# A retention layer and a wave MLP in one kernel: the whole instruction order redone, and q's scaling moved to the copy of x for six more units

## The chip, the cores and the metric

The kernel runs on one core of one Trainium2 chip. The metric is the device time of one execution in microseconds. Three executions of the kernel before gave 170.76, 172.34 and 173.16 us; the median is 172.34.

## The reference

`q`, `k`, `v` have the shape (4 batches, 8 heads, 768 tokens, 64) in float32. The first part is a recurrent retention, the second a mixing layer over its output:

```python
for t in range(S):                       # retention, gamma per head
    state = gamma * state + outer(k[t], v[t])
    y[t] = scale * (q[t] @ state)
x = y, heads side by side                # (4, 768, 512)
theta = x @ w_theta
zr, zi = x * cos(theta), x * sin(theta)
u = x + w_tok_r @ zr + w_tok_i @ zi      # over the 768 tokens of a batch
out = u + maximum(u @ w_ch, 0)
```

## The kernel before, in words

**Retention.** The work is cut into 24 units: unit n is one batch (n // 6), 256 tokens (the pair of 128-token chunks i = n // 2 % 3 of the batch) and four of the eight heads (h = n % 2). `Lk`, `Lq`, `Lv` (L159) load 256 KB each in float32, from SP's queue or ACT's as the last letter says (s or a), into 16 buffers for k and q and 9 for v. The decay is split: v is multiplied by gamma^-position when it is copied to bf16 (`cv`, L310), and the other factor, gamma^position times the scale, goes on q or on x. `ck` and `cq` are plain copies to bf16; `cqs` (L304) is the copy of q that scales it. If q was scaled, the result is copied to `xT` as it is (`XB`, L141 on DVE and L139 on ACT); if not, `XA` (L443, DVE alone) scales it there.

`Tk`, `Tq` (PE transposes, L318) with the copy `E`, or one DMA-transpose `Dk` (L334), give `kqT`. `A` (L348) is k.q within the 256 tokens, `m` (L357) its mask, `Y` (L425) the product with v, `ST` (L375) the unit's k.v sum, `S0` and `S1` (L393, L397) add it to the running state, `SB` copies the state to bf16 (`sbd`), and `I` (L413) applies the state of before to q. Units of one head half and batch depend on each other through the state.

**Mixing.** Two units give the `xT` of two 128-token chunks C = 0 to 23. `Tx` with the copy `Ex`, or a DMA-transpose `Dx` (L464), turns it to `x_sb`; `Hh` (L471) is x @ w_theta, `CN` (L478) its sine and cosine on ACT, `z` (L485) the two products. The six chunks of a batch must be there before `M` is complete: `M.t.s0` (L511) adds chunk s0 to the output tile t, two matmuls of 512 columns each. `u` (L518) adds x, `Tu` with `Eu`, or a DMA-transpose `Du` (L533), turns u, `O` (L538) multiplies by w_ch, `f` (L544) finishes the tile in one of four buffers, and `SO` (L549) stores it. The last tile is split in two halves (`Mh`, `uh`, `Tuh`, `Euh`, `Oh`, `fh`, `SOh`). The two token matrices are loaded by POOL in three groups of row blocks each (`Pw.r.g`, L184: block 0, blocks 1 and 2, blocks 3 to 5), and transposed on PE (`Tw.r.block`, L493) with the copy `Ew`; `Pth` and `Pch` load w_theta and w_ch. `Z` are matmuls on zeros whose result nobody reads; `const1` to `const9` and `constA` make tables, masks and the sine's table load (`const7`).

**What sets the order.** Nothing is scheduled at run time but by data. `ORDER` is a written list of 925 steps; the kernel calls them one after the other, and each engine (PE, DVE, ACT, POOL and SP, which issues transfers) executes its own instructions of them in that order. A step with a last letter p, v, a or s goes to POOL, DVE, ACT or SP's queue. A step waits until what it reads is there and its buffer is free, and all that stands behind it on the same engine waits with it. DMA-transposes are all issued by SP. The transfers that SP and ACT issue share eight completion counters in the order of the list, so each of them waits for the transfer eight places before it.

```python
    for token in ORDER:
        name, *args = token.split(".")
        ops[name](*(int(x) if x.isdigit() else x for x in args))
```

Of the kernel before, what the change touches and what calls it, by code (L numbers as in the profile page):

```python
# [27 lines left out]
Tk.1 E.1.a Y.0 ST.1 XB.0.1.a cqs.2.v Z.34 S0.1.v S1.1 cv.2.p SB.1.0.a Pth Lq.3.s Z.18 XB.0.0.v Tq.2  # L28
A.1 SB.1.1.a ck.2.a Tk.2 const7 I.1 Z.23 m.1 Y.1 XB.1.0.a Lk.3.s E.2.v XB.1.1.v A.2 ck.3.p m.2 ST.2
S0.2.v S1.2 SB.2.1.a Z.11 cqs.3.p Tq.3 Lv.3.s Tx.0 SB.2.0.a Lv.4.a Tk.3 E.3.a cv.3.v Z.3 I.2 cqs.4.v  # L30
Y.2 ST.3 S0.3.v XB.2.1.a ck.4.p A.3 XB.2.0.v Tk.4 Lk.5.s Tq.4 SB.3.0.p Ex.0.v Lq.5.s S1.3 Tx.1
# [4 lines left out]
Lv.6.s Tw.0.0 XA.5.1 z.2.v Tk.6 Hh.4 Hh.5 Lq.7.s Pw.1.1 Ew.0.0.a cv.6.v Tw.1.0 cqs.7.p E.6.a ST.6
z.3.v CN.4.1 Ew.1.0.v A.6 CN.4.0 CN.5.0 CN.5.1 ck.7.a Tx.5 Ex.5.v Tx.4 Ex.4.v M.0.3 Lv.7.a M.0.0
M.0.2 S0.6.v SB.6.1.a SB.6.0.p M.0.1 Lv.8.a Lk.9.a cv.7.p Tk.7 S1.6 z.5.v Pch Tq.7 E.7.a ck.9.p
z.4.v M.0.5 m.6 M.0.4 I.6 Tw.0.1 Ew.0.1.v Tw.1.1 Y.6 A.7 Lk.8.a Ew.1.1.v Tw.1.2 M.1.5 M.1.0 XA.6.1
# [18 lines left out]
m.13 cq.18.v u.9 Y.13 ck.15.p A.14 ST.14 S0.14.v M.8.0 SB.14.1.v ck.17.a ck.16.a Lq.19.a M.8.2 Tk.15
Lv.17.a Du.7 cv.15.p Lv.16.s XB.13.1.a XB.13.0.v SB.14.0.v M.8.5 S1.14 u.8 Tq.15 Hh.13 m.14 Tu.6
E.15.a I.14 Eu.6.v Hh.12 CN.13.1 cv.17.p CN.13.0 CN.12.0 Y.14 A.15 cv.16.p ST.15 M.10.5 cqs.17.v  # L60
XA.14.0 S0.15.v Dk.16 XA.14.1 cq.19.v SB.15.1.v M.10.1 M.10.0 Dx.13 SO.5.a M.10.2 SB.15.0.a M.10.4
CN.12.1 S1.15 O.6 cv.19.p m.15 Dx.12 I.15 M.10.3 Y.15 f.6 A.16 ST.16 Lv.18.a M.11.5 u.10 S0.16.v
m.16 Lk.20.a Dk.17 SB.16.0.p ck.18.a SB.16.1.a O.7 M.11.0 Du.8 M.11.3 f.7 z.13.v XB.15.0.a XB.15.1.a
# [572 lines left out]
```

## Time and profile before

| What | Value |
|---|---|
| times of three executions | 170.76, 172.34, 173.16 us; median 172.34 |
| the profiled execution's span | 169.0 us; no other time of it is recorded. The three executions lie 1.8 to 4.2 us above that span, the median 3.3 |
| granted TensorE clock | 1.00 |
| PE busy | 154.6 us (92%), 1992 matmuls |
| DVE, ACT, POOL busy | 123.6, 74.5, 66.7 us |
| DMA queues, share of 16 engines | SP's q1 53.6%, ACT's q10 30.3%, POOL's q0 12.8% |
| moved by DMA | 35.19 MB, mean 208 GB/s |
| instruction packets | q8 16 (0.26 MB), q14 7 (0.05 MB) |
| HBM | 25.69 MB read, 6.29 MB written |

Rows that the prediction uses, as mean or typical durations of one instruction:

| Step | Engine | us |
|---|---|---|
| cqs; cv | DVE; POOL | 0.68; 1.05 and 1.04 |
| ck, cq | DVE; ACT; POOL | 0.41; 0.61; 0.61 |
| XB; XA | DVE 0.41, ACT 0.37; DVE | 0.41 |
| SB | DVE; ACT; POOL | 0.29; 0.37; 0.39 |
| S0, S1 | DVE; ACT | 0.29 |
| E; Ex and Eu; Ew | DVE | 0.68; 0.41; 0.56 |
| E; Ex and Eu; Ew | ACT | 1.01; 0.59; 0.80 |
| z | DVE; POOL | 0.68; 2.12 |
| m; u; f | DVE | 1.22; 0.68; 0.68 |
| issue of a load; of a transpose | SP | 0.37 to 0.51; 1.2 |
| transfer, issue to landing (median) | k, q, v; transposes kqT, x, u; store | 4.4 to 5.7; 5.2, 4.0, 3.7; 3.1 |

Times in the profile count from the first instruction. An engine's "busy" is the sum of its instructions' spans; matmuls are pipelined, so PE's busy time is an upper bound on its work. The chain of waits is followed backwards from the last instruction; "issue" in it is time for which it shows no cause. A wait is put down to the engine or transfer whose signal came last.

### The profile page before, as it was taken

How to read it: one execution, taken by the hardware profiler on the slowest of the kernel's cores; microseconds unless marked ns; L12 is line 12 of the kernel's file. 1: busy time of each engine (PE TensorE's matmuls, PEld its weight loads, DVE VectorE, ACT ScalarE, POOL GpSimd, SP SyncE). 2: the span in 40 equal slices, each digit the busy share in tenths (PEclk: the TensorE clock that was granted, in tenths of full speed). 3: DMA queues.
4: the chain of work that ended last, by engine and by line, in shares of the span. 5: the costliest groups of instructions: out<-in, count | busy, mean ns of one | idle time of the engine just before them, and what ended most of it. 6: DMA issues, size and time to landing. Idle time of an engine off the chain costs nothing.

```text
span 169.0 us, 4878 instructions
## 1 busy us (share of the span) xinstructions
PE 154.6 (92%) x1992; PEld 85.9 (51%) x2022; DVE 123.6 (73%) x223; ACT 74.5 (44%) x133; POOL 66.7 (39%) x103
## 2 busy tenths in 40 slices
PE   5898768998999789999999999999999999999993
PEld 2355535655565445644455555554455544454561
DVE  3288969998478785976788998898968474343552
ACT  5965576964585445233008525761251423200010
POOL 7966049507421764150712830124816073500000
PEclk9999999999999999999999999999999999999999
DMA  4999998997999995899998999999999997333433
GB/s 124 296 290 248 292 242 154 162 220 209 197 210 203 222 263 172 214 256 211 318 280 204 177 245 217 278 273 193 197 320 158 222 215 157 126 93 93 124 126 127
DMA packets 70151, 35.19 MB, mean 208 GB/s; under 512 B 27505, under 2 KB 67185, under 8 KB 70129
## 3 DMA queue, kind: packets, MB, share of 16 engines
q1 hardware_dynamic: 45504, 18.23, 53.6%
q10 hardware_dynamic: 21936, 13.24, 30.3%
q0 software_dynamic: 2688, 3.41, 12.8%
q8 instruction: 16, 0.26, 0.7%
q14 instruction: 7, 0.05, 0.1%
HBM read 25.69 MB, written 6.29 MB: 189 GB/s over the span
## 4 chain that ended last, share of the span: by engine, by line
PE 54%; DMA 14%; DVE 10%; issue 6%; POOL 6%; ACT 6%; ACTq 1%; DVEq 0%; SPq 0%; POOLq 0%
PE y_ps L511 23%; DMA kqf<-in_k_dram 10%; PE o_ps L538 9%; PE th_ps L471 7%; DMA kqT<-kqb 4%; PE r_ps L425 3%; ACT cs L478 3%; DVE at L357 2%; PE at_ps L348 2%; PE kq_ps L318 2%; PE r_ps L413 2%; PE y_ps L563 2%; PE r_ps L375 1%; DVE z L485 1%; POOL kqb L141 1%
## 5 line engine op out<-in xcount | busy, mean ns | idle before, releaser
L511 PE MATMUL y_ps<-z,wtr 128*128 128x512 bf16 x130 | 49.3, 380 | 1.2 <-DVE z L485 0.3
L511 PE MATMUL y_ps<-z,wti 128*128 128x512 bf16 x129 | 48.9, 379 | 1.0 <-issue 0.8
L310 POOL TENSOR_TENSOR vb<-vf,vsc 128x512 bf16<-128x512 f32 x17 | 18.3, 1085 | 30.8 <-DMA vf<-in_v_dram 27.7
L357 DVE TENSOR_TENSOR at<-at_ps,mask 128x1024 bf16<-128x1024 f32 x24 | 29.2, 1218 | 0.8 <-PE at_ps L348 0.7
L518 DVE TENSOR_TENSOR u<-y_ps,x_sb 128x512 bf16<-128x512 f32 x23 | 15.8, 688 | 12.4 <-PE y_ps L511 10.2
L471 PE MATMUL th_ps<-wth,xT 128*128 128x512 bf16 x92 | 24.0, 379 | 0.3 <-DVE xT L141 0.2
L538 PE MATMUL o_ps<-wch,uT 128*128 128x512 bf16 x86 | 23.2, 380 | 0.6 <-DVE u L518 0.3
L478 ACT ACTIVATE cs<-th_ps,halfpi 128x512 bf16<-128x512 f32 x24 | 16.4, 686 | 12.5 <-PE th_ps L471 12.4
L511 PEld LDWEIGHTS <-wti 128*128 128x128 bf16 x138 | 13.5, 98 | 13.4 <-issue 1.2
L511 PEld LDWEIGHTS <-wtr 128*128 128x128 bf16 x138 | 13.5, 98 | 13.4 <-DVE wtr L141 0.5
L544 DVE SCALAR_TENSOR_TENSOR ot<-o_ps,u 128x512 f32<-128x512 f32 x23 | 15.8, 687 | 5.8 <-PE o_ps L538 5.7
L478 ACT ACTIVATE cs<-th_ps,zerob 128x512 bf16<-128x512 f32 x24 | 16.5, 686 | 7.4 <-PE th_ps L471 4.3
L141 POOL CAST kqb<-kqf 128x512 bf16<-128x512 f32 x19 | 14.8, 783 | 7.4 <-DMA kqf<-in_k_dram 6.9
L141 POOL CAST sbd<-s 64x256 bf16<-64x256 f32 (+1 forms) x14 | 5.0, 360 | 31.5 <-DVE s L393 24.1
L485 DVE TENSOR_TENSOR z<-cs,x_sb 128x1024 bf16<-128x1024 bf16 x18 | 13.9, 787 | 2.5 <-ACT cs L478 1.5
L485 POOL TENSOR_TENSOR z<-cs,x_sb 128x1024 bf16<-128x1024 bf16 x6 | 12.7, 2122 | 5.5 <-ACT cs L478 4.1
L139 ACT CAST sbd<-s 64x256 bf16<-64x256 f32 (+1 forms) x19 | 7.0, 370 | 16.1 <-DVE s L393 9.2
L139 ACT COPY kqT<-kq_ps 128x1024 bf16<-128x1024 bf16 x10 | 10.1, 1012 | 7.4 <-PE kq_ps L318 7.4
L471 PEld LDWEIGHTS <-xT 128*128 128x128 bf16 x96 | 8.6, 98 | 7.9 <-ACT xT L139 0.2
L538 PEld LDWEIGHTS <-uT 128*128 128x128 bf16 x92 | 8.4, 98 | 8.4 <-issue 0.4
L318 PE MATMUL kq_ps<-ident,kqb 128*128 128x128 bf16 x120 | 10.5, 220 | 2.0 <-POOL kqb L141 1.7
L318 PEld LDWEIGHTS <-kqb 128*128 128x128 bf16 x120 | 7.8, 98 | 6.0 <-POOL kqb L141 2.8
(77 smaller groups left out, 211.1 us busy)
## 6 DMA issues: line engine op xcount, KB each, us to landing
kqf<-in_q_dram ACTq DMA_DIRECT2D x14, 256.0 KB, 4.9
kqf<-in_k_dram ACTq DMA_DIRECT2D x12, 256.0 KB, 4.9
vf<-in_v_dram SPq DMA_DIRECT2D x12, 256.0 KB, 5.7
kqf<-in_k_dram SPq DMA_DIRECT2D x12, 256.0 KB, 5.0
vf<-in_v_dram ACTq DMA_DIRECT2D x12, 256.0 KB, 4.4
out_dram<-ot ACTq DMA_DIRECT2D x12, 256.0 KB, 3.1
out_dram<-ot SPq DMA_DIRECT2D x11, 256.0 KB, 3.0
kqf<-in_q_dram SPq DMA_DIRECT2D x10, 256.0 KB, 4.6
```

Of the source, the lines that this page charges most:

```text
L139: nc.scalar.copy(dst, src)
L141: engines[e].tensor_copy(dst, src)
L310: engines[e].tensor_mul(in_blocks(vb), by_token(raw["vf", n]), _bcast_last(K["vsc"][:, i, :, h * HU:(h + 1) * HU], D))
L318: nc.tensor.transpose(st["kq_ps", n][:, 4 * w + x, :], st["kqb", n][:, w, x * P:(x + 1) * P], K["ident"])
L357: nc.vector.tensor_mul(at.rearrange("p g j a t -> p (g j) (a t)"), st["at_ps", n].rearrange("p g j a t -> p (g j) (a t)"), _bcast_mid(K["m ...
L471: nc.tensor.matmul(th_ps, st["xT", C][:, j, :], K["wth"][:, j, :], start=(j == 0), stop=(j == 3))
L478: nc.scalar.activation(st["cs", C][:, w, :], st["th_ps", C], AF.Sin, bias=K["zerob" if w else "halfpi"], scale=1.0)
L485: engines[e].tensor_mul(st["z", b][:, c], st["cs", C], _bcast_mid(x_of(C), 2))
L511: nc.tensor.matmul(st["y", t], K["wT"][r][:, s0, t0 * P:(t0 + 1) * P], st["z", b][:, s0, r, :], start=(done == 0 and r == 0), stop=(done = ...
L518: nc.vector.tensor_add(st["u", t], st["y", t], st["x", b][:, t0, :])
L538: nc.tensor.matmul(o_ps, st["uT", t][:, j, :], K["wch"][:, j, :], start=(j == 0), stop=(j == nD - 1))
L544: nc.vector.scalar_tensor_tensor(st["ot", t], st["o", t], 0.0, st["u", t], ALU.max, ALU.add)
```

## The change

Only `ORDER` changes. It has the same 925 steps with the same meaning, in another order on every engine, and with other letters:

| Step | before | after |
|---|---|---|
| loads k, q, v issued by ACT / by SP | 38 / 34 | 17 / 55 |
| stores issued by ACT / by SP | 12 / 11 | 10 / 13 |
| q copied with scale (cqs) DVE / POOL | 8 / 7 | 1 / 8 |
| q copied plain (cq) ACT / POOL / DVE | 1 / 6 / 2 | 8 / 5 / 2 |
| k copied (ck) ACT / POOL / DVE | 9 / 13 / 2 | 9 / 7 / 8 |
| x copied plain (XB) ACT / DVE; scaled (XA) DVE | 16 / 14; 18 | 12 / 6; 30 |
| state to bf16 (SB) ACT / POOL / DVE | 19 / 14 / 15 | 27 / 13 / 8 |
| S0 ACT / DVE | 2 / 22 | 5 / 19 |
| kqT copies (E) ACT / DVE | 10 / 5 | 11 / 4 |
| x_sb: DMA-transposes; PE with copy ACT / DVE | 14; 4 / 6 | 13; 6 / 5 |
| uT: DMA-transposes; PE with copy ACT / DVE | 16; 3 / 4 | 17; 5 / 1 |
| weight copies (Ew) ACT / DVE | 6 / 6 | 5 / 7 |
| z POOL / DVE | 6 / 18 | 7 / 17 |

q's scaling moves to x for units 2, 3, 10, 16, 20, 21 and 23, and from x to q for unit 19. The nine units whose q and k are turned by DMA are the same (12, 13, 16, 17, 18, 20 to 23). The DMA-transposes stand at other places in the list relative to PE's steps. Unit 14's loads move ahead of the first M. `Pch` and the last two `Pw` stand behind `SB.7.0.p`, `cv.8.p`, `ck.9.p` and `cv.9.p` on POOL. The diff, cut to the lines of the list that hold these places:

```diff
 ORDER = """
-const2 Lv.0.s const1 const6.v Z.29 Z.2 const5 Z.38 Lk.0.a const3 Z.35 Z.8 Lq.0.s Lv.1.s Z.28 constA
-const4 Lq.1.a cqs.0.v const9 Lk.1.s cv.0.p Z.39 const8 ck.0.p Tk.0 Tq.0 ck.1.a E.0.v Lq.4.a ST.0
-Lk.4.a Z.15 A.0 cqs.1.p Tq.1 Lq.2.s S0.0.v SB.0.1.v Lk.2.s SB.0.0.p cv.1.p Lv.2.s S1.0 I.0 Z.27 m.0
...
-S0.2.v S1.2 SB.2.1.a Z.11 cqs.3.p Tq.3 Lv.3.s Tx.0 SB.2.0.a Lv.4.a Tk.3 E.3.a cv.3.v Z.3 I.2 cqs.4.v
...
-z.3.v CN.4.1 Ew.1.0.v A.6 CN.4.0 CN.5.0 CN.5.1 ck.7.a Tx.5 Ex.5.v Tx.4 Ex.4.v M.0.3 Lv.7.a M.0.0
-M.0.2 S0.6.v SB.6.1.a SB.6.0.p M.0.1 Lv.8.a Lk.9.a cv.7.p Tk.7 S1.6 z.5.v Pch Tq.7 E.7.a ck.9.p
...
-cq.8.p Lv.9.a XA.6.0 M.2.4 S0.7.a Lk.14.a SB.7.0.a SB.7.1.a Pw.1.2 cq.9.p S1.7 cv.8.v Tq.8 Tk.8
-M.2.2 I.7 M.2.5 Tu.0 E.8.a Y.7 u.1 A.8 ST.8 S0.8.v Pw.0.2 M.2.3 XB.7.1.v S1.8 SB.8.1.v Eu.0.a
...
-Tx.6 f.1 O.2 Ex.6.a ck.14.p Lk.10.s I.9 O.0 z.6.p m.9 Y.9 Tw.1.4 f.2 Tw.1.3 XA.9.1 Ew.1.4.v Hh.9
-cq.14.p Lv.10.s Tw.1.5 Ew.1.3.a Tk.14 Tq.14 f.0 XA.9.0 CN.9.1 Ew.1.5.v Hh.8 Tw.0.3 E.14.v cv.10.p
...
-SB.11.0.a Eu.3.a I.11 Lq.15.a Dk.12 M.5.1 f.4 Y.11 ck.13.p O.3 u.5 XB.11.0.v Du.5 Lk.15.a Hh.10
...
-CN.11.0 Ex.10.v z.10.v Lv.14.a M.7.3 cv.14.p M.7.0 M.7.2 M.6.2 Dx.11 M.6.3 M.6.4 SB.12.1.v M.7.1
-m.12 z.11.v SB.12.0.v Lq.18.a M.6.0 S1.12 cv.13.v Dk.13 M.6.1 M.6.5 cqs.16.p I.12 u.6 M.7.4 M.7.5
...
-XB.23.1.v z.20.p Du.14 O.14 u.17 SO.13.a Du.16 XB.23.0.a Dx.23 Dx.22 Du.17 M.21.1 O.15 f.14 z.21.p
...
-SO.15.s z.22.p M.18.1 M.18.3 M.19.1 M.19.0 M.19.4 f.16 O.17 M.18.2 u.19 M.18.0 M.18.5 Du.19 M.18.4
...
-Mh.1.0 M.20.4 SO.18.s M.20.0 O.22 f.22 M.20.5 M.20.3 M.20.1 M.20.2 u.20 O.21 Mh.1.3 Mh.1.4 Tu.20
-Mh.1.2 f.21 Mh.1.1 SO.22.a Tuh.0 SO.21.s Eu.20.v Euh.0 Mh.1.5 O.20 uh.1 Tuh.1 Euh.1 f.20 SO.20.a
-Oh.0 Oh.1 fh.0 Z.31 fh.1 SOh.0 SOh.1
+const1 const2 constA Lq.0.s Lv.0.s const3 const9 const5 Lk.0.s Z.34 Z.18 Lv.1.s Lk.1.s const4 ck.0.p
+Lq.1.s Lk.3.s Lk.2.s cv.0.v const6.v cqs.0.p Z.31 Lq.2.s Z.23 ST.0 S0.0.a Lq.3.s Lv.2.s Z.15 Tk.0
+Z.8 Lk.4.s ck.1.a const8 Lv.3.a Lq.4.a Lv.4.s Tq.0 Lk.5.s SB.0.1.v S1.0 cqs.1.p Z.38 Z.27 E.0.v A.0
...
+Ex.0.a ck.4.a A.3 Tx.1 I.2 Lq.6.s cv.3.p const7 Lk.7.s cqs.4.p Y.2 ST.3 m.3 S0.3.v SB.3.1.a SB.3.0.p
...
+Hh.3 E.6.a Lv.8.a I.5 Lk.14.a cv.6.p m.5 CN.3.1 CN.2.0 CN.3.0 Ex.3.v Tw.0.0 Ew.0.0.v Y.5 ST.6 A.6
...
+z.3.v CN.4.0 m.6 z.2.v CN.4.1 S0.6.a S1.6 z.4.v M.0.0 M.0.1 E.7.a M.0.2 Tx.5 Ew.0.2.v M.0.4 Ex.5.v
...
+S1.7 m.7 SB.7.0.p M.2.0 Tu.0 Pch Tq.8 Tk.8 E.8.v M.1.4 M.1.3 Eu.0.a XA.6.1 M.2.4 cv.8.p ck.9.p Tq.9
+I.7 A.8 Y.7 ST.8 u.1 S0.8.v M.2.1 cv.9.p Pw.1.2 XB.7.0.a Tk.9 M.2.2 Tx.6 SB.8.0.v m.8 XB.7.1.a
+SB.8.1.a M.2.3 M.2.5 Hh.6 u.2 Pw.0.2 E.9.a cq.14.a ck.14.a S1.8 Ex.6.v Tu.1 Hh.7 CN.6.1 Tk.14 I.8
+Eu.1.a CN.6.0 A.9 Y.8 ST.9 Tu.2 Dx.7 S0.9.v XA.8.1 Lq.10.s m.9 Lk.10.s z.6.p SB.9.0.v Lv.10.s CN.7.0
...
+XA.9.1 z.7.p Ew.1.5.a O.2 Tw.1.3 f.2 Ew.1.3.a Hh.9 Tw.0.3 Lq.11.s Tw.0.4 XA.9.0 Ew.0.4.v CN.9.0
...
+cv.11.v cv.12.v Lq.15.s Dx.8 Lv.13.s Dk.12 Lq.13.s m.10 SB.10.1.a SB.10.0.a Tq.11 M.5.4 M.3.0 I.10
...
+Dk.13 SO.0.s Lk.17.s Lk.18.s Lv.16.s M.6.3 S0.12.v S1.12 z.10.v Tq.15 CN.11.0 CN.11.1 SO.4.s M.6.0
+M.6.2 M.7.4 M.6.4 Lv.14.s Lk.16.s ck.15.p Tk.15 M.7.0 z.11.v SB.12.0.a SB.12.1.a M.7.1 Eu.5.v M.7.2
...
+Dx.22 Du.15 M.19.2 CN.23.0 CN.23.1 z.22.v Mh.0.4 O.16 O.15 Du.17 f.16 M.21.4 O.17 f.17 SO.16.s
...
+uh.0 M.18.2 M.22.5 SO.17.a M.19.1 M.22.2 M.19.5 M.18.3 M.22.3 Du.21 O.21 M.18.1 M.18.4 SO.14.a
...
+M.20.0 Mh.1.0 f.19 u.20 Du.18 Du.22 Mh.1.3 O.18 f.18 Tu.20 Mh.1.4 O.22 uh.1 SO.13.a Eu.20.a Tuh.1
+SO.19.s SO.15.s f.22 SO.18.s O.20 f.20 Euh.1 Euh.0 SO.22.s SO.20.a Oh.0 Oh.1 fh.0 Z.2 fh.1 SOh.0
...
 """.split()
```

More of the change, by code (lines that the diff above doesn't have):

```diff
@@ L58 @@
[L58 to L63, printed above, removed]
@@ new lines @@
+cq.20.p m.18 I.18 Tq.19 E.19.a Hh.16 M.13.1 M.13.3 A.19 Y.18 z.17.v ck.20.v Dk.20 ST.19 CN.16.0
+CN.16.1 z.16.v cv.20.p SO.10.s S0.19.a SB.19.1.a M.12.2 cq.21.a M.12.5 M.12.0 M.12.3 M.12.1
+SB.19.0.a Lv.22.s Lk.21.s XA.18.0 M.12.4 m.19 XA.18.1 M.13.4 u.12 M.13.5 M.13.0 Du.12 M.13.2 O.11
+S1.19 I.19 u.13 M.14.5 Y.19 ST.20 f.11 A.20 M.14.4 XB.19.1.v S0.20.v S1.20 SB.20.0.a XB.19.0.a
+Lk.22.s SB.20.1.a ck.21.v Lq.22.s Lv.21.s Hh.19 CN.19.0 m.20 CN.19.1 M.14.0 M.14.2 M.14.1 M.14.3
+cq.22.a cv.21.p Hh.18 u.14 ck.22.v Dk.21 Du.9 I.20 M.15.3 Dk.22 M.15.4 Y.20 ST.21 CN.18.0 CN.18.1
@@ L88 @@
+SO.19.s SO.15.s f.22 SO.18.s O.20 f.20 Euh.1 Euh.0 SO.22.s SO.20.a Oh.0 Oh.1 fh.0 Z.2 fh.1 SOh.0
+SOh.1
 """.split()
```

77 lines of the change are left out of this document (38 added, 39 removed).

## The prediction

> **What bounds the kernel now.** I read the busy shares first, then the windows by stage, then the chain of waits, then the DMA view of a stretch.
>
> ```profile
> PE 154.6 (92%) x1992; PEld 85.9 (51%) x2022; DVE 123.6 (73%) x223; ACT 74.5 (44%) x133; POOL 66.7 (39%) x103
> ```
>
> The windows by stage:
>
> ```profile
> 0.00:35.00 35.00, 28.22 (x480) 16.80 (x488) 26.43 (x53) 25.29 (x44) 21.37 (x53) 1.00 1.02 226
> 35.00:65.00 30.00, 27.48 (x361) 17.01 (x367) 23.37 (x41) 15.88 (x28) 13.89 (x18) 1.00 1.05 214
> 65.00:165.00 100.00, 97.82 (x1148) 51.57 (x1162) 72.81 (x128) 33.33 (x64) 31.48 (x33) 1.00 0.96 204
> ```
>
> In these the numbers are the stretch's length, PE's busy time, then PEld, DVE, ACT and POOL, and the last three are granted clock, DMA share and GB/s. PE is the bound: from 65 to 165 us it is idle for 2.2 us of 100. The idle time that a new order could win lies before: 6.8 us in the first 35 and 2.5 in the next 30. A busy PE also overstates the work done, since matmul ends are modelled. So I counted the work from the chain's durations: 138 matmul pairs of M (`y_ps`) at 0.43 us, 59.3; 24 groups of `th_ps` and 23 of `o_ps` at 0.86, 40.4; the attention matmuls of 24 units (0.22 + 0.35 + 0.25 + 0.22 or 0.11), 24.3; transposes, 14.3; 15 Z at 0.43, 6.5; the split last tile, 3.7: together 148. PE ends at 165.5, so 17 us are lost: 11.3 before the first M (34.5 us on the clock, 23.2 of work ordered ahead of it), 3.9 from there to unit 10's ST (65.85 us, 50.6 of work), 2.0 in the remaining 100 us.
>
> Why the start loses, by the chain (start, length, what):
>
> ```profile
> 18.89 0.39 POOL sbd L141
> 19.29 4.09 issue
> ...
> 23.42 1.05 POOL vb L310
> ...
> 43.86 10.72 DMA kqf<-in_k_dram
> 54.73 0.61 POOL kqb L141
> 55.34 2.08 POOL z L485
> 57.42 0.56 POOL kqb L141
> 58.03 0.40 PE kq_ps L318 x4
> ```
>
> The 4.09 us end with v of unit 4 landing: its load was issued by ACT at 16.73, and POOL sat waiting 4.13 us. The second hole is unit 14's k, which took 10.7 us to land, with z of chunk 6 and q's copy behind it on POOL; PE is busy 3.81 of 5 us from 55 and 4.46 from 60, so it costs 1.7 us.
>
> The thing that the change names is visible in the DMA view of 70 to 110 us, one slice a microsecond:
>
> ```profile
> DMA  8899997999999999999099999907999999379999
> GB/s 251 205 276 267 315 159 15 254 297 247 282 318 354 329 289 291 297 294 157 20 276 278 299 262 311 139 14 167 293 312 155 283 343 273 43 244 321 265 216 264
> ...
> q8 instruction: 4, 0.07, 0.8%
> ```
>
> Four times the rate falls from about 270 GB/s to 15-43 while the engines count as busy. PE's four instruction packets of this stretch (q8) start at 75.0, 86.5, 94.3 and 102.8 us, each 0.6 to 2 us ahead of a collapse, and a DMA-transpose is in flight at each. So the collision is real, over 1 us of DMA each. But who waits? PE is idle only 1.5 us in these 40 us. [...]
>
> **The change part by part.** The edit moves 925 steps and adds none.
>
> *q's scaling.* Units 2, 3, 10, 16, 20, 21, 23 take a plain copy of q and scale x; unit 19 goes the other way. On DVE four scaled copies go (0.68 each), eight x copies go (0.41), fourteen scaled x copies come (0.41), unit 19 adds 0.27 and frees 0.41: -2.7 - 3.3 + 5.7 - 0.1 = -0.4 us. POOL: three scaled copies (1.05) become plain copies (0.61) of other units: -1.3. ACT: four casts (0.61) come, six x copies (0.37) go, one comes: +0.6. PE: nothing. All of it lies beside PE's matmuls; with that cover gone, where ACT feeds PE directly, it would cost ACT's 0.6.
>
> *Engines reassigned.* Counting every step by its row, DVE falls 6 us in all (fewer scaled q, sbd and uT copies), ACT rises by 9.3 in compute (8 more sbd copies at 0.37, 7 more q casts at 0.61, 3 more s at 0.29, 2 more each of x_sb and uT at 0.59, less 1.3 for the rest). DVE is busy 73 of 100 us in the late stage, ACT 33, so this costs nothing there; it costs early, where ACT is busy 25.3 of 35 us and its steps ahead of the first M grow by 1.5.
>
> *Loads from ACT to SP.* 21 of 72 loads change queue; ACT keeps 17. An issue takes 0.37 to 0.51 us on either. [...] No run here shows one queue alone. What matters is the order: v4 is now the 15th load, behind no step of ACT. In the trace SP's issues released by the 1st and 14th landing stand at 5.06 and 15.80, 0.83 us a load, so v4 lands near 16.7 and not 23.4, and v5 (the 19th, with the 1 MB of `wth`, four loads' worth, between) near 23.3, against its use at 26.7 before. The most this can give is the whole 4.1 us. The least is nothing: ACT's steps before the first M, 27.6 us by rows, are nearly serial with the sines of chunks 0 to 4, and `const7`'s table load (1.28) stands between unit 3's state and its copy to sbd. I take **-1.0**, nearer the low end, because DVE (9.8 of 10) and ACT (8.1 of 10) are already almost full from 25 to 35 us.
>
> *The weight rows.* In POOL's queue `Pch` and the two last `Pw` now stand behind unit 7's sbd copy and cv.8, ck.9, cv.9 (0.39 + 1.04 + 0.61 + 1.04). Unit 7's ST ends at 27.7 of PE's work; DVE makes its state some 1.2 later (behind u.0 and a weight copy), and with 11.5 lost by then `Pch` starts near 41, the two `Pw` near 44.3 and 45.0 (before 40.06, 41.98, 43.26). Their rows gave 8.9 and 11.5 us to landing: 53.2 and 56.5. PE comes to their transposes at 40.8 and 44.0 of work, about 52.7 and 56: a stall of 0.5 to 1 where before there were some 4 us of slack. Bounds: nothing, if fewer loads compete, and 3 us if POOL runs late. I take **+1.0**. Unit 14's k and q are now loaded ahead of the first M and copied by ACT, so the hole at 55 to 62 goes; of its 1.7 us I count **-1.2**, since z of chunks 6 and 7 (2.12 each) now both go to POOL.
>
> *The late stage.* Collapses avoided are worth at most the 2.2 us of PE's idle time there. Against it: SP now issues loads behind transposes that wait. Behind Dk.13 stand k17, k18, v16, v14, k16; behind Dk.12 q13, k13, k15, q16. Of 1148 matmuls of this stage hardly one waits now, and every new order puts other steps next to each other: I take **+1.0**, bounds -2.2 and +5 (the rival below).
>
> *The tail.* After PE's end 3.5 us remain (165.5 to 169.0) in both. SO.13, SO.15 and their like are held back: five 256 KB stores fall in the last 5 us where before there were three, on two queues, at 3.1 us each to landing. O.15, O.17 and O.21 now directly follow transposes that need 3.7 us. I take **+0.5**, bounds 0 and +2.
>
> The sum: -1.0 + 1.0 - 1.2 + 1.0 + 0.5 = **+0.3**. The profile gives the execution's span, 169.0, and no other time of it; the median of the runs is 172.34, 3.3 above the span. I add the sum to the median: **172.6 us**. 2% (3.4 us) is about what a measurement can tell from no change; the shown runs spread over 2.4.
>
> **The rivals.** *Early loads pay in full.* If ACT isn't the bound, the 4.1 us of v4 and the 1.7 of unit 14 go and the weight rows arrive in time: 172.3 - 4.1 - 1.7 + 0.5 = 167.0. For it speaks that 5.8 us of PE waits are traced to exactly two late loads; against it, the full DVE and ACT at 25 to 35 us. Chance 0.20.
>
> *SP's queue holds loads back.* v14 and k16 are issued only after Dk.13, which waits for q and k of unit 13. Dk.13 is at 61.4 of PE's work, about 76 us; seven issues later, near 80, v14 goes out, and POOL wants it at 69.6 of work, about 84.6. With the median landing of 4.4 to 5.7 us this just holds; with the 10.7 us that unit 14's k took under the same DMA share (1.1 to 1.2), ST.14 is 5 us late and PE, in order, stands still with M ready behind it: 172.6 + 5 = 177.6. It decides from a landing of 5.5 us on. Before, POOL already waited 7.1 us for this very v (until 81.2) without PE noticing. Chance 0.23.
>
> *The collapses stay.* The order fixes who issues before whom, not when; a shift of 1 us puts a transpose on a fetch again. They cost PE at most 1.5 us in 40 before: 172.6 to 174. Chance 0.07, and the forecast 0.50; both within 2%.
>
> **How the numbers follow.** Faster by over 2% (under 168.9) 0.20, within 2% 0.55, slower (over 175.8) 0.25: the last is the second rival and a little for the bounds of the late stage and tail adding up. The range reaches to the middle of both rivals, **167.5 to 177.5**; the forecast's own is 169.5 to 175.5.
>
> **What would show it.** Right: first M at 33 to 34.5 us; no wait of POOL over 4 us before 24; a wait of PE of about 1 us for `row` near 53 to 57; DMA collapses of 70 to 110 us down to two or fewer; PE idle 3 us from 65 to 165. Wrong: the first M before 31, or a PE wait of several us behind v of unit 14.

## The result and the profile after

The changed kernel took 181.23 us in the median of five executions (180.49 to 183.82), the kernel before 172.34 beside it: 1.056 times as long, with a 95% interval from 1.047 to 1.065. The prediction was 172.6 with a range to 177.5, in effect no change, so it was wrong. Line numbers of the changed kernel are two lower than before (`M` is L509). The profiled execution is the longest of the five, 183.82 us with a span of 182.1. The two profiled spans, 169.0 and 182.1, lie 13.1 us apart and the two medians 8.9, so what this profile shows as lost is some 4 us more than the median loses. The ratios, here and below, leave disturbed executions out, so a median and a ratio can differ, and a kernel with too few undisturbed ones has no ratio.

The busy shares on the page of the kernel after:

```profile
PE 158.8 (87%) x1992; PEld 87.3 (48%) x2022; DVE 117.2 (64%) x211; ACT 83.4 (46%) x151; POOL 63.1 (35%) x97
```

The windows of the kernel after, in the columns of the prediction (length, PE, PEld, DVE, ACT, POOL, granted clock, DMA share, GB/s):

```profile
0.00:35.00 35.00, 26.53 (x458) 15.41 (x465) 22.60 (x43) 24.93 (x43) 20.13 (x55) 1.00 1.02 250
35.00:65.00 30.00, 28.31 (x375) 17.90 (x380) 21.19 (x42) 21.19 (x36) 11.85 (x13) 1.00 0.86 168
65.00:165.00 100.00, 90.18 (x1088) 46.98 (x1104) 66.07 (x115) 36.06 (x71) 31.10 (x31) 0.97 0.90 189
130.00:135.00 5.00, 2.26 (x59) 1.48 (x58) 1.71 (x5) 0.62 (x1) 0.00 (x0) 1.00 1.67 263
135.00:140.00 5.00, 4.95 (x15) 1.91 (x16) 3.14 (x6) 1.02 (x2) 2.48 (x2) 0.66 0.42 82
150.00:155.00 5.00, 2.24 (x11) 1.05 (x11) 2.77 (x2) 2.11 (x4) 2.11 (x1) 1.00 0.72 171
155.00:160.00 5.00, 4.70 (x15) 1.89 (x15) 0.94 (x2) 0.00 (x0) 0.00 (x0) 0.66 0.14 52
```

In the 100 us where PE was idle for 2.2 us it is now idle for 9.8. Two stretches of 5 us stand out, with PE busy for less than half of each, and behind each comes a stretch in which PE is busy but the granted clock is 0.66 on average (0.50 in the microseconds from 136 to 138 and from 156 to 159). So in this execution each of the two late waits is paid twice, with about 1.7 us more for the clock.

For a finer reading I use one sum in all that follows: **PE's waits up to a step** are the time of the step's first weight load less PE's work ordered ahead of it, as the prediction did for the first `M`. The work is counted at full clock, so the sum also holds what PE loses at a lower clock. A weight load can stand ahead of the wait of its matmul: M.16.3's first is at 132.11 us and its first matmul at 134.92. So by this sum a wait can show one step behind the step that waits: what is listed as M.16.5 is the wait of M.16.3, O.16 that of Mh.0.4, A.21 that of ST.21.

| up to | before | after |
|---|---|---|
| first M | 11.5 us | 16.1 us |
| unit 8's ST | 12.6 | 16.3 |
| unit 13's ST | 16.1 | 17.1 |
| unit 15's ST | 16.2 | 17.1 |
| unit 20's ST | 17.0 | 19.4 |
| unit 23's ST | 17.2 | 25.2 |
| O of tile 20 | 17.3 | 30.2 |

The start loses 4.6 us more than before, the middle wins 3.6 of them back, and at unit 15's ST, with half of the time gone, the two kernels are 0.9 apart. Then the changed kernel loses 13.1 us where the one before loses 1.1. The chain of waits of the kernel after (start, length, what) shows the two largest pieces of that (pieces of `issue` under 0.1 us are left out):

```profile
126.79 0.62 SPq L332
127.47 0.57 SPq L157
128.08 0.52 SPq L157
128.65 5.43 DMA out_dram<-ot
134.18 0.70 DVE ot L542
134.92 0.38 PE y_ps L509
...
148.22 0.70 DVE ot L542
148.93 1.22 SPq L462
150.20 2.62 DMA x_sb<-xT
152.91 2.35 DVE z L483
155.30 0.38 PE y_ps L561 x2
```

The first piece: VectorE can't write the result tile of f.9 until one of the four `ot` buffers has been stored; it stands for 3.29 us until 134.18. The store that frees it, SO.11, stands on SP behind a transpose (L332) and two loads (L157), and then takes 5.43 us. Until f.9 has read its bank, M.16.3, the first matmul of tile 16, has none to write, and PE stands for 2.74 us. The new order puts the stores of f.3 and f.5 58 and 52 us of PE's work behind the tiles, so two of the four buffers are out of use all that time. The second piece: the DMA-transpose Dx.22 is issued late, `z` of chunk 22 follows it, and the next step of PE, Mh.0.4, reads that `z`; Dx.22 stands only 0.4 us of PE's work ahead of that reader, where before there were 7.3.

The DMA view of 70 to 110 us in the kernel after, a slice a microsecond:

```profile
DMA  9799999919989989999999299899998689997999
GB/s 282 138 284 227 266 308 302 226 10 166 329 200 325 238 291 331 312 324 279 255 193 44 45 310 278 145 41 279 324 127 192 139 221 287 268 8 149 171 335 369
```

The rate still falls to 8-45 GB/s four times, as often as before. The instruction packets of this stretch on q8 (put down to PE, which has 4014 of the page's 4867 instructions) start at 77.4, 88.3, 95.2 and 104.7 us. Three falls begin within 1 us behind a packet with a transpose in flight, and the one at 91 to 93 us stands 3 us behind its packet. The change doesn't keep transposes and instruction packets apart in time.

### The profile page after: what moved, and what is told of

It is laid out like the page before. It is cut to its first block, busy times and chain, and to the rows that moved or that the text cites. A ratio compares the mean times of both kernels' runs of the same rounds, so it can differ in the third digit from the quotient of the medians.

```text
span 182.1 us, 4867 instructions
## 1 busy us (share of the span) xinstructions
PE 158.8 (87%) x1992; PEld 87.3 (48%) x2022; DVE 117.2 (64%) x211; ACT 83.4 (46%) x151; POOL 63.1 (35%) x97
## 3 DMA queue, kind: packets, MB, share of 16 engines
q0 software_dynamic: 2688, 3.41, 11.5%
## 5 line engine op out<-in xcount | busy, mean ns | idle before, releaser
L509 PE MATMUL y_ps<-z,wtr 128*128 128x512 bf16 x129 | 49.7, 385 | 3.1 <-DVE ot L542 2.7
L509 PE MATMUL y_ps<-z,wti 128*128 128x512 bf16 x131 | 50.4, 385 | 1.0 <-issue 0.8
L536 PE MATMUL o_ps<-wch,uT 128*128 128x512 bf16 x88 | 25.1, 408 | 1.2 <-ACT cs L476 0.6
L483 POOL TENSOR_TENSOR z<-cs,x_sb 128x1024 bf16<-128x1024 bf16 x7 | 14.8, 2121 | 20.3 <-DMA x_sb<-xT 11.6
L476 ACT ACTIVATE cs<-th_ps,halfpi 128x512 bf16<-128x512 f32 x24 | 16.1, 686 | 11.2 <-PE th_ps L469 8.2
L509 PEld LDWEIGHTS <-wti 128*128 128x128 bf16 x138 | 13.7, 99 | 14.9 <-issue 3.5
L476 ACT ACTIVATE cs<-th_ps,zerob 128x512 bf16<-128x512 f32 x24 | 16.5, 686 | 9.2 <-PE th_ps L469 8.7
L509 PEld LDWEIGHTS <-wtr 128*128 128x128 bf16 x138 | 13.6, 99 | 13.3 <-issue 1.1
L483 DVE TENSOR_TENSOR z<-cs,x_sb 128x1024 bf16<-128x1024 bf16 x17 | 14.7, 864 | 7.6 <-DMA x_sb<-xT 4.9
L139 POOL CAST sbd<-s 64x256 bf16<-64x256 f32 (+1 forms) x13 | 4.8, 373 | 41.1 <-DVE s L391 19.1
L137 ACT CAST sbd<-s 64x256 bf16<-64x256 f32 (+1 forms) x27 | 10.2, 378 | 16.3 <-DVE s L391 15.5
L536 PEld LDWEIGHTS <-uT 128*128 128x128 bf16 x92 | 9.2, 103 | 11.4 <-issue 3.7
L137 ACT COPY uT<-u_ps 128x512 bf16<-128x512 bf16 x5 | 3.0, 591 | 24.3 <-PE u_ps L521 24.2
L137 ACT COPY kqT<-kq_ps 128x1024 bf16<-128x1024 bf16 x11 | 11.2, 1018 | 5.5 <-PE kq_ps L316 5.5
L137 ACT CAST kqb<-kqf 128x512 bf16<-128x512 f32 x17 | 10.3, 621 | 7.4 <-DMA kqf<-in_k_dram 5.3
L316 PE MATMUL kq_ps<-ident,kqb 128*128 128x128 bf16 x120 | 11.6, 226 | 2.2 <-issue 1.3
```

Of the source, the lines that this page charges most:

```text
L137: nc.scalar.copy(dst, src)
L139: engines[e].tensor_copy(dst, src)
L316: nc.tensor.transpose(st["kq_ps", n][:, 4 * w + x, :], st["kqb", n][:, w, x * P:(x + 1) * P], K["ident"])
L476: nc.scalar.activation(st["cs", C][:, w, :], st["th_ps", C], AF.Sin, bias=K["zerob" if w else "halfpi"], scale=1.0)
L483: engines[e].tensor_mul(st["z", b][:, c], st["cs", C], _bcast_mid(x_of(C), 2))
L509: nc.tensor.matmul(st["y", t], K["wT"][r][:, s0, t0 * P:(t0 + 1) * P], st["z", b][:, s0, r, :], start=(done == 0 and r == 0), stop=(done = ...
```

## Experiments

"Waits" are PE's waits as above in each kernel's profiled execution, "late" is what is added to them behind unit 15's ST, and "span" is the length of that one execution. A time lies some 1.7 us above the span of its own execution (178.26 and 176.6 in e2), so with these 1.7 us added a profile can be set beside its kernel's median: it lies 2 to 4 us above it in after, e7, h4 and b5, and 2 to 3 below it in e5 and h2. Ratios are to the kernel before on the same chip.

| Kernel | median us | ratio (95%) | span | waits to ST.15 | late |
|---|---|---|---|---|---|
| before | 172.34 | | 169.0 | 16.2 | 1.1 |
| after | 181.23 | 1.056 (1.047 to 1.065) | 182.1 | 17.1 | 13.1 |
| e1_ot5 | 181.08 | | 178.6 | 17.7 | 8.9 |
| e2_dx | 177.76 | 1.036 (1.030 to 1.042) | 176.6 | 16.3 | 8.5 |
| e3_both | 177.49 | | 174.9 | 15.8 | 7.2 |
| e4_three | 178.95 | 1.036 (1.027 to 1.045) | 177.9 | 16.0 | 9.9 |
| e5_loads | 177.14 | 1.026 (1.019 to 1.032) | 173.4 | 15.6 | 5.9 |
| e6_so11 | 181.21 | 1.043 (1.034 to 1.053) | 180.6 | 16.0 | 12.6 |
| e7_unscale | 187.36 | 1.082 (1.073 to 1.090) | 188.8 | 17.6 | 19.2 |
| h1_a_then_b | 179.66 | 1.047 (1.039 to 1.055) | 178.8 | 16.3 | 10.1 |
| h2_b_then_a | 182.08 | 1.048 (1.036 to 1.061) | 177.3 | 16.7 | 8.2 |
| h3_a_then_b8 | 175.27 | 1.014 (1.006 to 1.023) | 174.4 | 21.7 | 0.6 |
| h4_b_then_a8 | 185.75 | | 188.1 | 21.8 | 13.9 |
| h5_bab | 177.54 | 1.027 (1.022 to 1.033) | 176.5 | 22.5 | 1.3 |
| h6_ab15 | 173.68 | 1.008 (1.003 to 1.012) | 172.0 | 16.5 | 3.6 |
| b1_dx22 | 172.47 | 1.004 (0.998 to 1.009) | 169.8 | 17.3 | 0.9 |
| b3_scale | 174.69 | 1.012 (1.006 to 1.017) | 173.4 | 18.7 | 3.2 |
| b4_early | 171.96 | 1.000 (0.995 to 1.005) | 168.5 | 16.0 | 0.9 |
| b5_late | 172.85 | 1.013 (1.007 to 1.018) | 173.5 | 19.1 | 2.7 |
| b6_v | 174.00 | 1.022 (1.016 to 1.028) | 171.2 | 17.5 | 2.0 |

### Where the loss is made: half of one order, half of the other

> The changed kernel's list up to ST.15, then what is left in the order of the kernel before (unit 16 keeps q unscaled, so its XA stays). At ST.15 PE stands 0.9 us later than before. Theory 1 (the loss arises behind ST.15): 172.3 + 0.9 = about 173 us. Theory 3 (the late start): 172.3 + 4.5 = about 177.

> The reverse: the list of the kernel before up to ST.15, then what is left in the changed kernel's order (unit 16 keeps q scaled, so its XB stays). Theory 1 (the loss arises behind ST.15): 181.2 - 0.9 = about 180.3 us. Theory 3 (the late start): 181.2 - 4.5 = about 176.7.

```diff
 h1:  ... cqs.17.p ST.15      (as after)
+     Z.2 SO.1.s SO.3.a cq.18.v ...   (the steps left, as before)
 h2:  the same with the two lists exchanged
```

Both made new waits where the lists join. In h1, VectorE stands still for a load that the changed list had not issued yet:

```profile
DVE kqb L139 <- DMA kqf<-in_q_dram: 8.5, 1, 8.5
```

PE's waits jump by 9.5 us from unit 15's ST to unit 18's, and only 0.55 us come behind that. So the end of the order of before, once past the seam, costs nothing in this kernel either. The total alone, 179.7, would have been read as a loss that is kept from the start. h2 has a seam of its own (a load of v, 3.3 us at I.15); behind it 4.9 us are lost, but at M.15.4 (1.7), A.21 (0.9) and A.23 (1.7), and neither at M.16.5 nor at O.16. So the changed order loses time there in other places too when its transfers fall otherwise.

> The changed kernel's list to ST.15 with the loads q19 and v19 issued right behind Lq.18 (so that the seam of the first joined kernel, a wait for q19, is not there), then what is left in the order of the kernel before. PE's waits up to ST.15 sum to 15.6 to 17.1 us in the runs with the changed start, 16.2 in the kernel before, whose order adds 1.1 us behind it. Theory L (all of the loss is made behind ST.15): 171.7 to 173.2 us. Theory S (some of it is made earlier and only shows late): 176 or more.

```diff
-Lq.18.a XB.13.1.a
+Lq.18.a Lq.19.a Lv.19.a XB.13.1.a
```

With q19 and v19 issued in time the same join gives 173.68 us, 1.008 of before. **Seven and a half of the 8.9 us lie behind unit 15's ST.** With the order the joined list also takes back the moved scaling of units 19 to 23, so a part of the 7.5 can be the scaling's; it is priced below in the order of before alone. The time is 0.5 us above the upper end of what was expected, and two waits were left: 1.5 us for a transpose of u at O.6 and 1.3 us for one of unit 20 at A.20. The window of this kernel (columns as above) against the 90.18 of the changed one and the 97.82 of before:

```profile
65.00:165.00 100.00, 96.24 (x1128) 49.98 (x1144) 69.25 (x122) 34.18 (x65) 34.23 (x36) 1.00 0.95 204
```

### What becomes of the late start

> The changed kernel's list up to ST.8, then what is left in the order of the kernel before. At ST.8 PE stands 3.7 us later than in the kernel before (waits summed: 16.33 against 12.60 us), and the kernel before loses 3.6 us more up to ST.15. The first cut at ST.15 made a seam (cq.19 waited 8.5 us for a load that the changed list had not issued); at ST.8 no load is missing. Theory S (the start's loss is kept): 172.3 + 3.7 = 176. Theory G (what ends the waits from ST.8 to ST.15 is given by loads and queues, not by when the start ended, so that the late start is given back): 172.5 to 173.5.

> The reverse: the list of the kernel before up to ST.8, then what is left in the changed kernel's order. Theory S (losses add): PE's waits sum to 12.6 + 0.8 = 13.4 us at ST.15, 2.8 us less than in the kernel before, and the end is at 181.2 - 3.7 = 177.5 us. Theory G: some 16.5 us at ST.15 and 180 to 181 us at the end. By both the late waits at A.21, M.16.5 and Mh.0.4 with O.16 stay.

> Start of the kernel before (its list to ST.8, with q14 issued next to k14), middle of the changed kernel (to ST.13, with q17 and q18 issued near v14), end of the kernel before. PE's waits by stage in the two profiles: 12.6 us up to ST.8 in the kernel before, 0.8 us from there to ST.13 in the changed one (3.5 us in the kernel before), 1.2 us behind ST.13 in the kernel before. Theory S (losses add): 14.6 us instead of 17.35, so 172.3 - 2.7 = 169.6 us. Theory G (the middle's waits are given by when loads and weight rows arrive, so the changed list lost little there only because it came late): 172 to 173. A new seam would make it slower.

```diff
 h3:  after to ST.8, then before      h4:  before to ST.8, then after
 h5:  before to ST.8 (Lq.14.a next to Lk.14.a), after to ST.13
      (Lq.18.a Lq.17.a next to Lv.14.s), then before
```

In h3, with the changed start, the waits grow by 0.9 us from ST.8 to unit 10's ST, where the order of before alone grows by 2.6: part of the late start is given back, as theory G has it. Then a wait of 3.9 us comes at I.12 and Y.12: VectorE stands at a `z` for a DMA-transpose that took 6.62 us from issue to landing and was issued close to its reader, and the state that I.12 reads is made behind that `z`:

```profile
76.54 0.72 PE th_ps L469 x4
77.26 6.62 DMA x_sb<-xT
```

The total, 175.27, is therefore near theory S for another reason. Behind ST.15 h3 loses 0.6 us.

With the start of before, the middle of the changed order is no longer cheap: in h4 and h5 PE's waits grow by 6.7 and 6.8 us from ST.8 to ST.13, half of it at Tk.14. In h5 the chain shows why (`issue` left out):

```profile
46.50 0.13 ACTq L157
46.67 8.85 DMA kqf<-in_q_dram
55.60 1.15 ACT kqb L137 x2
```

q of unit 14 comes 8.85 us after its issue, among the weight rows. In h4 it is k of unit 14, with 9.08 us. The changed kernel issues both loads well before its late first `M` (q lands at 38.1 us, k at 42.8), and its DMA is idle from 43 to 46. Both starts also lost more than the same list in before: 15.1 us up to ST.8 and not 12.5, with a wait of 2.5 to 2.8 us at ST.4 for v of unit 4 (1.2 before) and 3.4 us at half clock soon behind it (the clock of the whole execution is 0.964 in h4 and 0.979 in h5). So h4 met neither theory (21.8 us at ST.15; S had 13.4 and G 16.5), and h5 was slower as with a new seam. The loss at the start and the gain in the middle did not add in them, as theory G has it, but a seam at unit 14 would look the same, and what decides is not shown. The 169.6 us of theory S weren't reached.

### What makes the late waits

> The changed kernel with five `ot` buffers in place of four, its order untouched. Theory 1 (held result buffers): two of the four are held by f.3 and f.5, whose stores are far behind in the list, so f.9 waits 5.3 us for the store SO.11 behind two transposes and two loads on SP, PE waits 2.6 us for the bank at M.16.5, and the clock is at a half for 3.4 us after it (1.7 us more). With a fifth buffer both go: 181.2 - 4.3 = 176.9 us, at most 176.4 with the 0.5 us near 109 us. Theory 2 (SP's queue as such: what is late is late because SP blocks, and the next wait on the same queue takes over): 180.5 to 181.5. Theory 3 (start: the 4.5 us by which the first M is late is never won back): 181.

```diff
-st["ot", t] = work.tile([P, dm], FT, name="ot", bufs=4)
+st["ot", t] = work.tile([P, dm], FT, name="ot", bufs=5)
```

The wait of M.16.5 for f.9 is gone from the trace, and PE's waits from unit 20's ST to unit 23's fall from 5.8 to 1.9 us. That held buffers make this wait is shown. The time is not settled: four executions gave 178.1 to 184.7, with the median where it was. What is left in e1 is the second wait (the view of waits; engine, line, what it waited for, sum, times, longest):

```profile
PE y_ps L561 <- DVE z L483: 3.0, 1, 3.0
```

> The changed kernel with the one store SO.11 issued on ScalarE's queue in place of SP's, at its place in the list; four `ot` buffers as before. Theory Q (the store is late because SP has a transpose and two loads to issue ahead of it, 126.1 to 128.7 us): f.9 waits about 2.6 us less, PE's wait at M.16.5 goes from 2.6 us to under 0.5, the half clock behind it goes, 181.2 - 3.9 = 177.3 us. Theory B (only the number of buffers matters): no change.

```diff
-SO.8.a ck.23.a SO.11.s
+SO.8.a ck.23.a SO.11.a
```

PE's wait at M.16.5 goes from 2.6 to 1.06 us and the clock stays at full behind it. But f.9 no longer waited for SO.11; it waited for SO.8, issued by ACT at 128.56 us, as early as SP issued SO.11 in the changed kernel (128.65), and landed after 3.83 us and not after 5.43 (in the changed kernel SO.8 landed at 133.68, 0.4 us ahead of SO.11):

```profile
132.48 0.69 DVE L542 SCALAR_TENSOR_TENSOR ot<-o_ps,u 128x512 f32<-128x512 f32 x1 [1.75 <-DMA out_dram<-ot]
```

SO.11 itself went out later, at 132.21, behind ck.23 on ACT. So the run shows that another buffer came free sooner, and not what SP's queue cost. The median didn't move (181.21), and the ratios, 1.043 and 1.056, overlap in their intervals: in the profiled execution the wait of Mh.0.4 (O.16) took 3.86 us, with a half clock of 6.8 us behind it (0.962 over the whole execution), so there what was won at the first wait was lost again at the second.

> The changed kernel with the DMA-transposes Dx.21, Dx.22 and Dx.23 issued earlier in SP's list (21 right behind Dx.20, 22 behind XA.23.0, 23 behind XA.23.1), so that they no longer stand behind the store SO.5. Theory 1 (late order): z.22 waits for Dx.22 until 152.9 us, PE 3.3 us for z.22, and half a clock after it costs 1.7 us; both go: 181.2 - 5.0 = 176.2 us. If z.22, z.23 on VectorE and GpSimd side by side (2.34 us instead of 0.7) are what is late, half of it stays: 178.5. Theory 3 (start): no change, 181.

```diff
-Du.14 Dx.20 A.23 ... XA.23.0 M.17.0 ... SO.5.s Mh.0.2 Dx.23 Dx.22
+Du.14 Dx.20 Dx.21 A.23 ... XA.23.0 Dx.22 M.17.0 O.14 XA.23.1 Dx.23 ... SO.5.s Mh.0.2
```

3.5 of the expected 5.0 us came: the wait of 3.3 us is down to 1.3 at O.15. The first wait is still there, so it does not come from the second:

```profile
DVE ot L542 <- DMA out_dram<-ot: 8.5, 5, 2.9
PE y_ps L509 <- DVE ot L542: 2.7, 2, 2.4
DVE z L483 <- DMA x_sb<-xT: 2.5, 3, 1.2
```

> The changed kernel with both edits: five `ot` buffers, and Dx.21 to Dx.23 issued earlier. The earlier transposes alone gave 177.8 us, with PE still waiting 2.25 us at M.16.5 for a result buffer. Theory 1 (two independent late waits): that wait and the slower clock behind it go as well, 177.8 - 2.3 = 175.5 us, or 174 with the clock. Theory 2 (SP's queue as such, the next late step takes over): 177 to 178.

> As the kernel with five buffers and the three earlier transposes, and ck.21 behind S1.19 and Dk.21 behind f.11, so that 7 us of PE's work instead of 1.7 us lie between Dk.21 and its reader A.21. Theory 1 (each late wait is a step whose transfer is issued less than its own duration ahead of its reader): the 1.2 to 1.8 us for which A.21 waits in all four runs go too: 1.2 to 1.8 us below the kernel with two edits. Theory 2: no change against it.

> The changed kernel with five `ot` buffers, the earlier Dx.21 to Dx.23, the loads k21 and v21 issued behind Lv.20, v23 behind Lq.22, then ck.21 behind S1.19 and Dk.21 behind f.11. In the runs so far A.21 and ST.21 waited 1.2 to 2.4 us because v21 is loaded 4.9 us of PE's work ahead of its reader ST.21 (12.9 us in the kernel before) and such a load takes 5.2 to 5.5 us; moving ck.21 alone made VectorE wait for k21 instead (Y.19 late by 3.4 us). Theory 1 (late issues, three places): no wait over 1 us from ST.15 to the last O, 172 to 174 us. Theory 2 (SP's queue as such): the next transfer on SP is late in their place, 176 to 178 us.

```diff
 e3:  e1 and e2
 e4:  e3;  S1.19 ck.21.v I.19 ... ST.20 f.11 Dk.21 A.20
 e5:  e4;  Lv.20.s Lk.21.s Lv.21.s Tx.17 ... Lq.22.s Lv.23.a Hh.19
```

e3's best execution took 173.5 us, its others 176.6 to 180.7. The median, 177.5, is the number of theory 2, no better than e2's 177.8, but the spread of 7 us leaves the choice open. Its profile still has 2.1 us at A.21, where ST.21 waits for the load of v21. e4 was a miss: with the copy of k21 ahead of u.13 on VectorE, VectorE stood still for 3.3 us, u.13 came late, and PE waited 3.4 us ahead of Y.19 instead. With the loads earlier as well (e5) late waits are 5.9 us, the lowest of the changed order though in a profile 1.9 us below its median, at 1.026 of before. The expected 172 to 174 did not come. The rest is spread over I.21 and Hh.21 (1.2 us each), A.18, Hh.17 and others; I have not separated it.

### One late step in the order of before

> The kernel before with one step made late as the change has it: Dx.22 and z.22 (on VectorE) right ahead of M.19.4, the first reader of z.22 (0.0 us of PE's work between Dx.22 and that reader instead of 7.3). Theory 1: PE waits 3.3 us there, and the clock falls to a half for 3.4 us behind it, 1.7 us: 172.3 + 3.3 to 5.0 = 175.6 to 177.3. Theory 2 (only a queue that is full of loads makes it late; there are none here): 172.3 to 173.

```diff
-Du.16 XB.23.0.a Dx.23 Dx.22 Du.17 ... SO.15.s z.22.p ... M.19.0 M.19.4
+Du.16 XB.23.0.a Dx.23 Du.17 ... SO.15.s ... M.19.0 Dx.22 z.22.v M.19.4
```

No change: 1.004 (0.998 to 1.009). The theory that nearness in the list decides falls. SP's own instructions tell why:

```profile
142.88 0.47 SPq L549 DMA_DIRECT2D out_dram<-ot  x1
143.40 1.23 SPq L464 DMA_TRANSPOSE x_sb<-xT  x1
149.35 1.19 SPq L533 DMA_TRANSPOSE uT<-u  x1
```

SP runs ahead of PE. It issued Dx.22 at 143.4, and then stood free for 4.7 us, though in the list Dx.22 stands right ahead of its reader. In the changed kernel SP was held at Du.16 until 141.0, and then had SO.3, Du.14, Dx.20, Dx.21, SO.5 and Dx.23 to issue at 0.6 to 1.9 us each, with Dx.22 the last, at 150.2. What counts is when SP comes to a step, not how near the step is written to its reader.

> The kernel before with the loads v21 and v23 as late as in the changed order: 5.1 us of PE's work ahead of ST.21 and 3.8 us ahead of ST.23 (12.9 and 21.9 before), their copies behind them on GpSimd. Theory 1 (a load takes 5.2 to 5.5 us and its copy 1.0 us, so a reader that near waits): 1.3 to 2.5 us at ST.21 and as much or more at ST.23, 175 to 177 us. Theory 2 (SP runs ahead of PE, so the place in the list is not the time, as with the late Dx.22): 172.3 to 173.

```diff
-Lv.20.s Dk.20 CN.16.0 Lv.21.s ...  O.11 Lv.23.s Lk.21.a
+S0.20.v Lv.21.s ... cv.22.p cv.21.p ...  M.16.3 Lv.23.s ... Y.22 SO.0.a cv.23.p
```

1.022, but only 0.9 us of it lies behind unit 15's ST, and the wait it was made for is 0.65 us:

```profile
121.71 3.50 DMA vf<-in_v_dram
125.35 1.05 POOL vb L310
126.76 1.40 PE y_ps L511 x6
```

v21 landed in 3.5 us instead of 5.4. The other waits are at Tu.2 (1.85 us), a place where this list is the same as that of before. Five kernels with the same list up to unit 10's ST (before, b1, b5, b6 and h2, whose edits all lie later) stand there at 15.2 to 17.0 us. So up to two microseconds between two profiles can come from the middle without an edit there, and the late load is neither shown nor excluded as a cause of its own.

### The scaling of q

> The kernel before with the second half of the change done alone: units 2, 3, 10, 16, 20, 21, 23 copy q unscaled and scale the copy of x on VectorE (XA), unit 19 the other way round; every step stays where it is. By the prediction this is hidden beside PE: 172.3, at most 0.5 us either way. Rival: VectorE is late in the seven units' XA (two of 0.35 us each where ScalarE had some of the XB): up to 173.5.

> The kernel before with the moved scaling of units 2, 3 and 10 alone. In the run with all units the largest new wait was at Tu.2 (2.3 us, behind cv.9 and the load of v9, which took 9.8 us), before unit 10. If that wait comes from the early units: 174.3 us. If the early units are hidden and that load was late by itself: 172.3.

> The kernel before with the moved scaling of units 16, 19, 20, 21 and 23 alone. In the run with all units A.20 and I.21 were late by 0.6 us each, and PE's waits behind ST.15 summed to 3.2 us instead of 1.1. If VectorE's added XA (two of 0.4 us in units 16, 20, 21, 23 where ScalarE had some of the copies) are late there: 173.3 to 174.3 us. If hidden: 172.3.

```diff
 b3:  both;   b4 (units 2, 3, 10):          b5 (units 16, 19, 20, 21, 23):
-     cqs.2.v  XB.2.1.a XB.2.0.v            cqs.20.v  XB.20.1.a XB.20.0.a
+     cq.2.v   XA.2.1   XA.2.0              cq.20.v   XA.20.1   XA.20.0
```

The three early units cost nothing (1.000, within 0.5%). The late ones cost 1.3% (0.7 to 1.8), which agrees with b3's 1.2%. Late waits grow from 1.1 to 2.7 us, in b3 to 3.2, at A.20 and I.21; b5's profile lies 2.4 us above its median. The part of b5 that shows behind ST.15 is 1.6 us; the rest lies mostly upstream of the edit and can't be laid to it.

> The changed order with the scaling of q put back as it was: units 2, 3, 10, 16, 20, 21, 23 scale q in its copy (on the engine that the kernel before uses) and copy x unscaled, unit 19 the other way round. Done alone in the order of before, the moved scaling cost 2.2 us (0.6 to 1.7%). If it costs the same here: 181.2 - 2.2 = 179 us. If the waits behind ST.15 cover it: 181. If GpSimd's and VectorE's longer scaled copies (1.0 us instead of 0.8, 0.68 instead of 0.43) are late at the start instead: 182.

```diff
-cq.20.p ... XA.20.1 XA.20.0
+cqs.20.v ... XB.20.1.a XB.20.0.a        (units 2, 3, 10, 16, 19, 21, 23 likewise)
```

This was not a clean reverse: the scaled copies stand on VectorE and GpSimd in these kernels, where the changed order has plain copies on ScalarE too, so with the scaling the engine changed. VectorE now stood ahead of the scaled copy of q20 until its load came:

```profile
113.70 4.59 DMA kqf<-in_q_dram
118.33 0.04 issue
118.38 0.16 DVE kqb L302
```

and PE waited 2.95 us at Y.18. The run says nothing of the scaling itself; it shows what a step that waits for a load costs on the engine that feeds PE.

## Why the prediction was wrong, step by step

**The start, -1.0.** Measured +4.6 at the first `M` (39.4 us on the clock instead of 33 to 34.5). The ten kernels with this start stand there at 14.5 to 16.1 us of waits, the seven with the start of before at 11.5 to 14.3, five of them under 12.2, so 3 to 4.5 us is the usual loss. What 21 loads from ACT to SP do to the rate no run shows by itself; over the first 35 us it was 250 GB/s, and 226 before. The step that failed is the choice of v4's load as what bounds the start. That load came in time: no wait of POOL for a load before 24 us was over 1.4 us. But I priced only v4, and not the first units' copies. ST.0 waits 2.8 us for POOL's copy of k0, now the third load on SP, and the loss grows behind it: at ST.3 the waits are 12.1 us against 7.2. A copy that the new order puts on VectorE beside two of POOL took 2.38 us instead of the 0.68 of its row, though 1.37 in e2 and h6:

```profile
17.22 2.38 DVE L308 TENSOR_TENSOR vb<-vf,vsc 128x512 bf16<-128x512 f32 x1
```

PE's matmuls also ran longer for more of the start; the windows, with 1.00 for the granted clock there, do not show it, but the durations do. The same four matmuls of `Z` took 1.91 us near 10.5 us here and 1.04 near 11.3 us before (the first line is of the kernel after). With its matmuls nearly twice as long PE stood at two `Z` until A.0 at 12.35, while the kqT that A.0 reads was written by 11.44:

```profile
10.51 1.91 PE L278 MATMUL zz<-zero 128*128 128x512 bf16 x4
11.25 1.04 PE L280 MATMUL zz<-zero 128*128 128x512 bf16 x4
```

**The weight rows, +1.0, and unit 14, -1.2.** PE's wait for `row` was 0.2 us. The hole at 55 to 62 did go: from the first `M` to ST.13 the changed kernel loses 1.0 us, the one before 4.6. The mechanism was right and the size too small. But h4 and h5 did not get this gain with the early start, so I take start and middle as one term, +0.9 at ST.15 where I had -1.2 for the three. That is within what kernels with the same list differ by there: 15.6 to 17.7 us with the start and middle of after, 16.1 to 17.4 in before, b1, b6 and h2.

**q's scaling, nothing.** Wrong for the late units, +1.3% in the order of before. I counted engine time beside PE and found it covered. The XA of units 20 to 23 stand on VectorE between the mask and the states, and at I.21 PE waits for those. (A.20 waited for a transpose of 7.4 us, which need not be the edit's.)

**The late stage, +1.0 within -2.2 and +5, and the tail, +0.5 within 0 and +2.** This is where the prediction fell: 8.1 us lost from unit 15's ST to unit 23's, where the order of before loses 1.0, and 5.0 behind it against 0.1. I searched the list for one late load (v14 behind Dk.13) and took a guess for all others. v14 did no harm. By the medians h6 puts 7.5 us behind ST.15, the scaling of units 19 to 23 included; the earlier transposes took off 3.5 of it (e2) and all edits together 4.1 (e5), and where the rest arises stays open. The numbers to find the others stood in the list: two of four `ot` buffers held for 52 and 58 us of work, Dx.22 0.4 us ahead of Mh.0.4, v21 4.9 and v23 3.2 us of work ahead of their ST (12.9 and 21.9 before). b1 shows that such a number is a suspect and no verdict. For the tail I named O.15, O.17 and O.21 behind their transposes; what waited in the changed kernel was Mh.0.4.

**The rivals.** SP's queue did hold transfers back, the second rival's mechanism, but at 126 to 155 us and not for v14. Its 177.6 us was the nearest of the forecasts, for the wrong transfer. What it cost is not separated: the two waits with their half clocks make 9.3 us in the profiled execution, and the edits against both gave 3.7 us of the median (e3). "The collapses stay" held as well (four in 70 to 110 us, I said two or fewer), and they are not what moved the time: PE is idle for 1.9 us of these 40, and for 1.5 before.

**The clock.** Not in my sum at all. After PE's waits of 2.6 us at M.16.5 and 3.3 us at O.16 the granted clock was 0.66 over 5 us each, which is 3.4 us at a half, about 1.7 us more per wait; in windows of half a us it is 1.00 up to 135.5 and 156.0 us, 0.6 to 0.7 us after PE has gone on, 0.50 to 0.59 from there, and 1.00 again from 139.0 and 159.5. e1's wait of 3.28 us did not set it off. Nor did one of 3.31 us in h2 (1.00 from 97 to 110 us, and over the whole execution), while behind waits of 2.1 us in e3 and 2.3 in b3 the granted clock was 0.57 over 4 us (0.980 and 0.988 over the whole executions). So the length of a wait alone does not decide, and what does is not shown.

No kernel here beats the one before; the best with parts of the new order is h6, 0.8% behind it.

## What to carry to other kernels

In a list that PE follows without a wait, an average of idle time says little of what another order costs. Before pricing a reorder, go through every transfer: on which queue is it issued, what stands ahead of it there and waits, and when will the queue come to it; and count at each allocation how many buffers of the pool are held by stores that come late. When two orders are joined to find a loss, look for the seam's own wait before believing the total, and split PE's waits by stage rather than compare two times.

## What the runs showed of the hardware that was not expected

A VectorE copy of 128x512 float32 with two inputs took 2.38 us beside POOL's operations of the same kind, and `z` on VectorE 2.35 us (0.69 alone) while POOL made the other `z`. POOL's own instructions there took 1.03, 1.03 and 2.11 us, as elsewhere (1.04 and 2.12). In these three places the time added to VectorE's is about the overlap and not a factor: the copy of 2.38 us (1.70 more than 0.68) ran beside POOL's for 1.85 us, the `z` of 2.35 us (1.66 more) for 1.79, and a `z` of 1.55 us in the kernel before (at 30.99; 0.87 more than 0.68) beside one of POOL's scaled copies for 0.99. One overlap of 0.54 us (at 81.02 before) added nothing to VectorE's copy of 0.68, but POOL's took 1.44 us and not 1.04. What in the two engines makes this is not shown. The second late wait contains such a place (152.91 in the chain), so those 1.66 us are a part of its price.

A DMA-transpose took 6.62 us from issue to landing (h3, with an instruction packet of q8 starting at 77.3 us beside it) where Dx.22 in the kernel after needed 2.62. The rate falls to 19-29 GB/s from 78.5 to 80 us there. In this one place a late transpose cost PE 3.9 us, though from 70 to 110 us before, with four such falls, PE was idle for 1.5 us in all; how much of the 6.62 us the fall made is not shown, for loads and another transpose were in flight too.
